# Four neighbouring heads to a chunk: q in one transfer, k in one and its last keys at the end of the tile

## The chip, the cores and the metric

The kernel runs on one core of one Trainium2 chip. The metric is the device time of one execution in microseconds. Several executions are timed; one more is recorded by the profiler, and the profile's numbers come from that one.

## What is computed

Attention with normalised q and k, and behind it two matrix products with a tanh-approximated GELU between them:

```python
q, k, v: (8, 12, 448, 64) float32        # batches, heads, positions, head size
q_n, k_n = rmsnorm(q, g_q), rmsnorm(k, g_k)
scores = q_n @ k_n.T / sqrt(64);  attn = softmax(scores)
x = (attn @ v).transpose(0, 2, 1, 3).reshape(3584, 768)
out = gelu_tanh(x @ w_in) @ w_out        # w_in (768, 2048), w_out (2048, 768)
```

## The kernel before

The work goes batch by batch. A batch has 12 heads, taken as three chunks of four heads; a chunk is two pairs of heads, and pair `hp = 2c + j` of chunk `c` is its even (`j = 0`) or odd (`j = 1`) pair. `head(c, j)` says which heads these are: before, heads 2c and 2c+1 for the even pair and 6+2c and 7+2c for the odd one.

For each chunk the kernel loads q and k (`load_q`, `load_k`, `loads`), squares them (`square`), sums the squares (`total`), makes the reciprocal root (`rsqrt`), scales (`normed`) and transposes. In q 112 partitions hold four positions each. Of k's 448 keys the first 384 lie three to a partition, and the last 64 are kept apart: those of the even pair on partitions 0 to 63, those of the odd pair on 64 to 127, in one place ("slot") of the tile. So a k tile holds 2 × 7 units of 64 numbers on each partition: three for each of the two even heads, three for each of the two odd heads, and the two last ones. v is loaded in the same split: `vb` holds the first 384 keys, `vr` the last 64, in two halves of 64 partitions (`load_v` parts 1 and 2) whose other half stays zero.

In batch 0 and for the first chunks of batch 1 TensorE transposes; later chunks are transposed by DMA (`dma_trans`, lines 281 and 285), and k is then multiplied by the product of the two gains (`gain`, line 291, on VectorE). Scores go to PSUM, ScalarE takes the exponential (L343), VectorE adds exponentials over key tiles (`key_sum`, L355 and L357), TensorE sums over keys with a matrix of ones and multiplies by v (L443, `x_couple` and `sums_couple`), and the normalised result lands in `xT`, one 128-row slab per pair. `mm1` multiplies `xT` by `win`; since pairs are not in the order of the model's columns, the slab of w_in for pair `c` is `c // 2 + NCH * (c % 2)`. GELU follows (L537), and `mm2` multiplies by `wout` (L443 and L557) and stores.

Every engine works through its queue in the order in which the program names the instructions. This order is written by hand. `FRONT` is the order up to the middle of batch 0's first product: `v1`, `v2`, `v0` load batch 0's v; `V0` to `V2` batch 1's; `w0` to `w3` the quarters of w_in; `o0` to `o3` those of w_out; `nq0:P` scales q of pair 0 on GpSimd, and so on. Behind it `STEPS` gives, batch by batch, the order of TensorE's work; while batch b's first product runs, batch b+1 is scaled on GpSimd and transposed, and the next loads are issued, at numbered places of that product:

```python
m1 += [(-1, lambda c=c: normed_all(b + 1, c)),
       (4 * c + 4, lambda c=c: transposed(b + 1, c))]
m1 += [(9, lambda: gain(b + 1, 0)), (13, lambda: gain(b + 1, 1))]
m1 += [(2, lambda: loads(b + 2, 1)), (6, lambda: loads(b + 2, 2))]
```

So on SyncE's queue, which also issues the stores, there stand in this order: loads (b+2, chunk 1), transposes of q and k (b+1, chunk 0), loads (b+2, chunk 2), transposes (b+1, chunk 1), transposes (b+1, chunk 2). GpSimd's queue holds the loads of v and of the weights beside its scaling and squaring; `load_v_piece` brings a later batch's v in five pieces, the last two of which are the halves of `vr`.

Of the kernel before, what the change touches and what calls it, by code (L numbers as in the profile page):

```python
# [8 lines left out]
F32 = mybir.dt.float32  # L9
# [3 lines left out]
AX = mybir.AxisListType  # L13
# [3 lines left out]
def kernel(  # L17
# [23 lines left out]
    NK = 3  # L41
# [68 lines left out]
        return slice(0, NK) if j == 0 else slice(NK, NS)  # L110

    def head(c, j):
        return 2 * c + HP * j

    def load_q(b, c):
        t = rawqk.tile([P, CH, NQ, D], F32, tag="rawq", name="rawq")
        raws["q", b, c] = t
        return [
            lambda j=j: nc.sync.dma_start(  # L119
                t[:, 2 * j:2 * j + 2],  # L120
                q[b, head(c, j):head(c, j) + 2].rearrange("h (p t) d -> p h t d", t=NQ),
            )
            for j in range(2)
        ]

    SM = 128 * NK

    def own(j):
        return slice(64 * j, 64 * j + 64)

    def load_k(b, c):
        t = rawqk.tile([128, 2, NS, D], F32, tag="rawk", name="rawk")
        raws["k", b, c] = t

        def main(j):
            h = head(c, j)
            nc.sync.dma_start(
                t[:, :, 4 * j:4 * j + NK],
                k[b, h:h + 2, :SM].rearrange("a (p t) d -> p a t d", t=NK),
            )  # L140

        def last(j):
            h = head(c, j)
            nc.sync.dma_start(t[own(j), :, NK], k[b, h:h + 2, SM:].rearrange("a p d -> p a d"))  # L144
        return [lambda: main(0), lambda: main(1), lambda: last(0), lambda: last(1)]

    def loads(b, c):
        lq, lk = load_q(b, c), load_k(b, c)
        for go in (lq[0], lk[0], lq[1], *lk[1:]):
            go()  # L150

    def load_v(b, part):
        if part == 0:
            nc.gpsimd.dma_start(
                vb[b % 2].rearrange("p h t d -> p h (t d)"),
                v[b, :, :SM].rearrange("h (p t) d -> p h (t d)", t=NK),
            )
        else:
            j = part - 1
            nc.gpsimd.dma_start(  # L160
                vr[b % 2][own(j), j], v[b, HP * j:HP * j + HP, SM:].rearrange("h p d -> p h d")
            )

    def load_v_piece(b, i):

# [6 lines left out]
            v[b, hs, :SM].rearrange("h (p t) d -> p h (t d)", t=NK),  # L172
        )

    def view(n, t, j=None):

        if n == "q":
            return t if j is None else t[:, 2 * j:2 * j + 2]
        return t if j is None else t[:, :, slots(j)]

    def sq_tile(n, flat):
        if n == "q":
            return flat[:P].rearrange("p (h t d) -> p h t d", h=CH, t=NQ)
        return flat[:, :2 * NS * D].rearrange("p (a s d) -> p a s d", a=2, s=NS)

    def square(b, c, n, eng, part=None):
        if (n, b, c) not in sqs:
            sqs[n, b, c] = sq_tile(n, sqp.tile([128, CH * NQ * D], F32, tag="sq", name="sq"))
        sq, raw = sqs[n, b, c], raws[n, b, c]
        if part is not None:  # L190
            if part[0] == "pair":
                sq, raw = view(n, sq, part[1]), view(n, raw, part[1])
            elif n == "q":
                sq, raw = view(n, sq, part[1]), view(n, raw, part[1])
            else:
                sq, raw = sq[:, part[1]], raw[:, part[1]]
# [5 lines left out]
    def stat(t, b, c, n, j=None):  # L202

        if b == 0:
            ns = NQ if n == "q" else NK + j
            at = 14 * j + (0 if n == "q" else 8)
            return t[:P if n == "q" else 128, c, at:at + 2 * ns].rearrange("p (a t) -> p a t", a=2)
        if n == "q":
            s = t[:P, c, :CH * NQ].rearrange("p (h t) -> p h t", h=CH)
            return s if j is None else s[:, 2 * j:2 * j + 2]  # L210
        s = t[:, c, CH * NQ:].rearrange("p (a s) -> p a s", a=2)
        return s if j is None else s[:, :, slots(j)]

    def total(b, c, n, j=None):
        nc.vector.reduce_sum(stat(ssq[b % 3], b, c, n, j), view(n, sqs[n, b, c], j), axis=AX.X)  # L215

    def rsqrt(b, c=slice(0, NCH), at=slice(0, NU)):
        if b not in rinvs:
# [12 lines left out]
    def normed(b, c, n, j, eng):  # L231
        if (n, b, c) not in nrms:
            shape = [P, 2, NQ, 2, D] if n == "q" else [128, NS, 2, D]
            nrms[n, b, c] = nrmp.tile(shape, BF16, tag=f"nrm{n}", name=f"nrm{n}")
        t = nrms[n, b, c]
        dst = t[:, j] if n == "q" else t[:, slots(j)]
        r = stat(rinvs[b], b, c, n, j)
        eng.tensor_mul(  # L238
            dst.rearrange("p t a d -> p a t d"), view(n, raws[n, b, c], j),
            r.to_broadcast(list(r.shape) + [D]),  # L240
        )

    def trans(b, hp, n, pool, tag=None):
        c, j = hp // 2, hp % 2
# [67 lines left out]
    def scores(b, hp, t, parts=1):  # L312

        c, j = hp // 2, hp % 2
        sc = place("sc")
        if t == "r":
            exrs[b, c] = exr.tile([128, 2, S], BF16, tag="exr", name="exr")
            for a in range(2):
                for jj in range(2):
                    r = slice(a * D, (a + 1) * D)  # L320
                    o = slice(64 * jj, 64 * jj + 64)
                    nc.tensor.matmul(  # L322
                        sc[o, a, :S], kT[r, c, NK, o], qT[b][r, 2 * c + jj],
                        start=True, stop=True,
                    )
            dst = exrs[b, c]
        else:
            if t == 0:
# [33 lines left out]
    def pair_products(b, hp, what, home=None, part=None):  # L362
# [5 lines left out]
        main = [exs[b, hp][:, t] for t in range(NK)]  # L368
        if what:
            steps = [(main[t], lambda a, t=t: vb[b % 2][:, head(c, j) + a, t]) for t in range(NK)]  # L370
            steps.append((exrs[b, c], lambda a: vr[b % 2][:, j, 2 * c + a]))
        elif b == 0:
            steps = [(e, lambda a: ones) for e in main] + [(exrs[b, c], lambda a: onesr[:, j])]
        else:
            steps = [(ess[b, hp], lambda a: ones)]
        if part is not None and j:
# [108 lines left out]
    def mm1_couple(b, fs, apart):  # L485
# [29 lines left out]
    def mm1(b, fs, cs=range(HP), parts=1, only=None, act=True):  # L515
# [8 lines left out]
        for j, f in enumerate(fs):  # L524
            m = 128 // parts
            for c in cs if only in (None, f) else ():
                for i in range(parts):
                    nc.tensor.matmul(  # L528
                        h[i * m:(i + 1) * m, j, :S],
                        win[:, c // 2 + NCH * (c % 2), f * 128 + i * m:f * 128 + (i + 1) * m], xT[b][:, c],  # L530
                        start=(c == 0), stop=(c == HP - 1),
                    )
        if cs[-1] == HP - 1 and only in (None, fs[-1]) and act:
# [282 lines left out]
    def front(step):  # L816
# [93 lines left out]
        y1 tpk0 v0 nq1:P ck0:D shift cq0:D s0 sq3:A e0 y3 s1 tq2 tq3 tk2 nk1:P L11 e1 y3 tpk1  # L910
        tpq1 s2 sk3:P w0 e2 ck1:D cq1:D tk3 y1 y1 s3 y3 y4 s4 sa0 rS1 nq2:P e3 sk4:A e4 sq4:D
        nk2:D s5 sb0 tpq2 s6 tpk2 tq4 tk4 st0 cq2:D rc0 ck2:D e5 sq5:P nk3:P nq3:D L12 e6 sa1 s7
        tpk3 tpq3 s8 sb1 e7 rs4 s9 xa0 sk5:P ck3:D rb0 cq3:D tk5 st1 e8 e9 xb0 s10 xt0 tq5 rc1
        rb1 nk4:P nq4:P e10 sa2 s11 rs5 e11 nk5:P nq5:P w1 xa1 sb2 xb1 s12 tpk4 tpq4 s13 Sq0:P
        Sk0:P e12 cq4:A st2 xt1 ck4:D rc2 rb2 e13 xa2 xb2 sa3 tpq5 tpk5 s14 e14 xt2 ck5:D cq5:D
        s15 xa3 sb3 e15 U xb3 s16 s17 s18 e16 st3 e17 rc3 rb3 xt3 e18 sa4 mb0 mb1 sb4 xa4 xb4
# [3 lines left out]
        Nq11:D Nk10:D Nq10:D Sq2:D Tk2 Tq2 Ck1:A g5 Cq1:A md6 md7 g6 g7 md8 g8  # L920
"""
    for step in FRONT.split():
        front(step)
# [174 lines left out]
```

## Time and profile before

| what | value |
|---|---|
| timed runs | 405.2, 405.5 and 404.85 us; median 405.2 |
| the profiled execution | 405.13 us, of which the span from the first to the last instruction is 403.3 |
| granted TensorE clock | 1.000 |
| TensorE busy | 392.3 us |
| ScalarE, VectorE, GpSimd busy | 305.6, 240.9, 138.4 us |
| moved by DMA | 54.65 MB |

The rows shown below come from several views. In the list of groups a row gives the line, engine, operation, what it writes and reads with its shape, the count, and after the bar the busy time in us and the mean duration in ns. In the order of time a row gives start and length in us; a bracket is the idle time ahead of it and what ended it. `SPq` is SyncE's queue issuing transfers. "DMA to landing" is the time from a transfer's issue until its data is there. A TensorE busy share near 100% does not by itself mean full speed, as the ends of matmuls are modelled; the count of matmuls in a stretch says more.

### The profile page before, as it was taken

What the parts mean: (1) busy time and instruction counts of PE and PEld (TensorE: products, weight loads), DVE (VectorE), ACT (ScalarE), POOL (GpSimd) and SP (SyncE); (2) the same over time, 40 slices, a digit from 0 to 9 for tenths busy, and PEclk for the clock granted to TensorE, in tenths of its full rate; (3) what the DMA queues carried; (4) which work ended last, traced back from release to release, by engine and by line L of the source; (5) the groups of instructions that cost most, each with busy time, mean ns of one, the idle gap of its engine ahead of it and who ended that gap; (6) DMA issues with size and microseconds to landing.
All of it is one profiled execution on the core that took longest, in us unless ns stands there. A gap on an engine that the chain in (4) does not pass through costs nothing.

```text
span 403.3 us, 17169 instructions
## 1 busy us (share of the span) xinstructions
PE 392.3 (97%) x7644; PEld 273.0 (68%) x7644; DVE 240.9 (60%) x406; ACT 305.6 (76%) x412; POOL 138.4 (34%) x155
## 2 busy tenths in 40 slices
PE   7899989999999999999999998999999999999996
PEld 3344557677777898766776666766787667966564
DVE  5989839987887437961498314973488411770010
ACT  4997889969997689885998479875998358964400
POOL 6878001252500764065603447037520740000000
PEclk9999999999999999999999999999999999999999
DMA  8999999998891599449981399918980290210022
GB/s 191 225 234 223 205 197 209 232 235 155 208 166 29 158 178 191 98 115 170 183 141 40 92 180 142 195 47 181 156 121 16 74 145 3 81 40 5 2 79 79
DMA packets 98090, 54.65 MB, mean 136 GB/s; under 512 B 63968, under 2 KB 94560, under 8 KB 98016
## 3 DMA queue, kind: packets, MB, share of 16 engines
q1 hardware_dynamic: 71392, 41.69, 47.3%
q0 software_dynamic: 26304, 11.80, 23.0%
q8 instruction: 59, 0.97, 1.0%
q14 instruction: 15, 0.12, 0.1%
q10 hardware_dynamic: 320, 0.07, 0.1%
HBM read 45.61 MB, written 11.01 MB: 140 GB/s over the span
## 4 chain that ended last, share of the span: by engine, by line
PE 88%; SPq 4%; DMA 2%; DVE 2%; ACT 2%; issue 1%; POOL 0%; ACTq 0%; DVEq 0%; POOLq 0%
PE hh L443 25%; PE om L443 16%; PE mm L443 12%; PE o L443 10%; PE sc L336 6%; PE o L557 5%; PE so L443 4%; PE hh L528 4%; PE ox L382 1%; DMA rawk<-in_k_dram 1%; DMA kT<-nrmk 1%; PE sc L322 1%; PE o L382 1%; SPq L285 1%; SPq L144 1%; SPq L119 1%
## 5 line engine op out<-in xcount | busy, mean ns | idle before, releaser
L343 ACT ACTIVATE ex<-sc,shift 128x896 bf16<-128x896 f32 x144 | 137.2, 1023 | 7.7 <-PE sc L336 6.2
L443 PE MATMUL hh<-xT,win 64*64 64x448 bf16 x2304 | 129.3, 349 | 0.0
L443 PEld LDWEIGHTS <-g 64*64 64x64 bf16 x3072 | 105.6, 107 | 27.4 <-issue 1.9
L443 PEld LDWEIGHTS <-win 64*64 64x64 bf16 x2688 | 87.0, 106 | 39.7 <-ACTq L452 10.3
L443 PE MATMUL om<-wout,g 64*64 64x384 bf16 x1664 | 105.0, 323 | 0.1
L443 PE MATMUL o<-wout,g 64*64 64x384 bf16 x704 | 83.0, 323 | 0.6 <-ACT g L537 0.6
L443 PE MATMUL mm<-wout,g 64*64 64x384 bf16 x704 | 83.2, 323 | 0.0
L537 ACT ACTIVATE g<-hh 128x896 bf16<-128x896 f32 x55 | 50.0, 916 | 26.3 <-PE hh L443 24.4
L215 DVE TENSOR_REDUCE ss<-sq 128x14 f32<-128x896 f32 (+4 forms) x45 | 47.8, 1078 | 19.3 <-ACT sq L198 16.9
L336 PE MATMUL sc<-qT,kT 64*64 64x448 bf16 (+1 forms) x540 | 54.8, 352 | 1.9 <-DVE qT L267 1.4
L238 POOL TENSOR_TENSOR nrmq<-rawq,rinv 112x512 bf16<-112x512 f32 x35 | 36.7, 1064 | 34.0 <-DMA qT<-nrmq 28.3
L291 DVE TENSOR_SCALAR kT<-kT,gcol 128x896 bf16<-128x896 bf16 x19 | 13.4, 707 | 51.5 <-DMA kT<-nrmk 51.5
L937 POOL COPY mark<-es 1x1 bf16<-1x1 bf16 x8 | 1.8, 225 | 115.3 <-DVE es L357 97.3
L238 POOL TENSOR_TENSOR nrmk<-rawk,rinv 128x512 bf16<-128x512 f32 (+1 forms) x34 | 31.8, 950 | 3.0 <-ACT rinv L224 2.1
L357 DVE TENSOR_TENSOR es<-ex 128x896 bf16<-128x896 bf16 x42 | 25.8, 614 | 11.7 <-ACT ex L343 11.7
L336 PEld LDWEIGHTS <-kT 64*64 64x64 bf16 (+1 forms) x540 | 23.5, 104 | 12.1 <-issue 4.1
L443 PE MATMUL o<-xT,win 64*64 64x448 bf16 x192 | 30.9, 349 | 0.0
L443 PE MATMUL mm<-xT,win 64*64 64x448 bf16 x192 | 30.9, 349 | 0.0
L357 DVE TENSOR_TENSOR es<-es,ex 128x896 bf16<-128x896 bf16 x42 | 26.0, 620 | 4.3 <-ACT ex L343 2.4
L343 ACT ACTIVATE exr<-sc,shift 128x896 bf16<-128x896 f32 x24 | 24.4, 1018 | 1.2 <-PE sc L322 1.0
L397 DVE STREAM_TRANSPOSE rb<-rc 128x448 f32<-128x448 f32 x34 | 21.9, 645 | 1.1
L443 PEld LDWEIGHTS <-vb 64*64 64x64 bf16 x504 | 16.6, 106 | 6.6 <-ACTq L452 0.8
(120 smaller groups left out, 525.6 us busy)
## 6 DMA issues: line engine op xcount, KB each, us to landing
rawq<-in_q_dram SPq DMA_DIRECT2D x48, 224.0 KB, 4.5
rawk<-in_k_dram SPq DMA_DIRECT2D x48, 192.0 KB, 4.9
vb<-in_v_dram POOLq DMA_DIRECT2D x18, 192.0 KB, 6.1
win<-in_moe_w_in_dram POOLq DMA_DIRECT2D x4, 768.0 KB, 10.8
wout<-in_moe_w_out_dram POOLq DMA_DIRECT2D x4, 768.0 KB, 19.6
out_dram<-osb SPq DMA_DIRECT2D x7, 336.0 KB, 3.4
out_dram<-osb SPq DMA_DIRECT2D x8, 288.0 KB, 2.8
out_dram<-osb SPq DMA_DIRECT2D x8, 240.0 KB, 2.6
```

What stands on the lines that cost most here:

```text
L215: nc.vector.reduce_sum(stat(ssq[b % 3], b, c, n, j), view(n, sqs[n, b, c], j), axis=AX.X)
L238: eng.tensor_mul(dst.rearrange("p t a d -> p a t d"), view(n, raws[n, b, c], j), r.to_broadcast(list(r.shape) + [D]),)
L291: nc.vector.tensor_scalar(kT[:, c], kT[:, c], gcol[:, 0:1], None, op0=ALU.mult)
L336: nc.tensor.matmul(sc[o, a, :S], kT[r, c, 4 * j + t, o], qT[b][r, hp], start=True, stop=True,)
L343: nc.scalar.activation(dst, sc[:, :, :S], AF.Exp, scale=scale, bias=shift)
L357: nc.vector.tensor_add(es, ex[:, 0] if t == 1 else es, ex[:, t])
L382: nc.tensor.matmul(o[a * D:(a + 1) * D], w(a), e[:, a], start=(i == 0), stop=(i + 1 == len(steps)),)
L397: nc.vector.transpose(oas["rb", hp], oas["rc"].to_broadcast([128, S // 32, 32]))
L443: self.last = nc.tensor.matmul(self.outs[k][own(m)], w, e, start=not self.begun[k], stop=self.left[k] == 0,)
L528: nc.tensor.matmul(h[i * m:(i + 1) * m, j, :S], win[:, c // 2 + NCH * (c % 2), f * 128 + i * m:f * 128 + (i + 1) * m], xT[b][:, c], start= ...
L537: nc.scalar.activation(g[:, fs[0]:fs[0] + len(fs), (b % 2) * S:(b % 2 + 1) * S], hs1[fs[0]][:, :, :S], AF.Gelu_apprx_tanh)
L557: nc.tensor.matmul(o[j * m:(j + 1) * m, :HD], g[:, f, i * 128 + j * m:i * 128 + (j + 1) * m], wout[:, f, half * HD:(half + 1) * HD], start ...
```

## The change

A chunk becomes four neighbouring heads, 4c to 4c+3, and pairs are now in the order of the model's columns, so `mm1` takes slab `c` of w_in. From batch 1 on, q of a chunk is one transfer instead of two, and the first 384 keys of k are one instead of two; the last keys remain two transfers and land behind the others at the end of the tile. Batch 0 keeps the two halves and its old layout. Tiles of raw values, squares and sums are addressed as flat runs of units (`units`, `flat`). As the last keys are no longer between the others, `normed` scales the odd pair's k from batch 1 on in two instructions (384 and 128 elements on a partition) instead of one of 512. The halves of `vr` take every second head of a chunk, so each half is loaded by two transfers instead of one. In `FRONT`, `v1` and `v2` move to the front of the order, and `V0 V1 V2` move behind `o2 o3`.

```diff
     def head(c, j):
-        return 2 * c + HP * j
+        return CH * c + 2 * j
...
     def load_q(b, c):
         t = rawqk.tile([P, CH, NQ, D], F32, tag="rawq", name="rawq")
         raws["q", b, c] = t
-        return [
-            lambda j=j: nc.sync.dma_start(
-                t[:, 2 * j:2 * j + 2],
-                q[b, head(c, j):head(c, j) + 2].rearrange("h (p t) d -> p h t d", t=NQ),
+
+        def some(lo, hi):
+            h = head(c, 0)
+            nc.sync.dma_start(
+                t[:, lo:hi], q[b, h + lo:h + hi].rearrange("h (p t) d -> p h t d", t=NQ)
             )
-            for j in range(2)
-        ]
+        return some
...
     def load_k(b, c):
-        t = rawqk.tile([128, 2, NS, D], F32, tag="rawk", name="rawk")
+        t = rawqk.tile([128, 2 * NS, D], F32, tag="rawk", name="rawk")
         raws["k", b, c] = t
+        odd = t[:, 2 * NK:].rearrange("p (a t) d -> p a t d", a=2)
+
+        def main(lo, hi):
+            h = head(c, 0)
+            dst = t[:, NK * lo:NK * hi].rearrange("p (a t) d -> p a (t d)", t=NK)
+            if (lo, hi) == (2, 4):
+                dst = odd[:, :, 1:].rearrange("p a t d -> p a (t d)")
+            nc.sync.dma_start(
+                dst, k[b, h + lo:h + hi, :SM].rearrange("a (p t) d -> p a (t d)", t=NK),
+            )
+
+        def last(j):
             h = head(c, j)
             nc.sync.dma_start(
-                t[:, :, 4 * j:4 * j + NK],
-                k[b, h:h + 2, :SM].rearrange("a (p t) d -> p a t d", t=NK),
+                odd[own(j), :, 0] if b == 0 else t[own(j), NK * CH:],
+                k[b, h:h + 2, SM:].rearrange("a p d -> p a d"),
             )
...
     def loads(b, c):
-        lq, lk = load_q(b, c), load_k(b, c)
-        for go in (lq[0], lk[0], lq[1], *lk[1:]):
-            go()
+        some, (main, last) = load_q(b, c), load_k(b, c)
+        for lo, hi in ((0, 2), (2, 4)) if b == 0 else ((0, 4),):
+            some(lo, hi)
+            main(lo, hi)
+        for j in range(2):
+            last(j)
...
             j = part - 1
-            nc.gpsimd.dma_start(
-                vr[b % 2][own(j), j], v[b, HP * j:HP * j + HP, SM:].rearrange("h p d -> p h d")
-            )
+            for a in range(2):
+                nc.gpsimd.dma_start(
+                    vr[b % 2][own(j), j].rearrange("p (c a) d -> p c a d", a=2)[:, :, a],
+                    v[b].rearrange("(c h) s d -> h c s d", h=CH)[2 * j + a, :, SM:].rearrange(
+                        "c p d -> p c d"),
+                )
...
-        t = nrms[n, b, c]
-        dst = t[:, j] if n == "q" else t[:, slots(j)]
-        r = stat(rinvs[b], b, c, n, j)
-        eng.tensor_mul(
-            dst.rearrange("p t a d -> p a t d"), view(n, raws[n, b, c], j),
-            r.to_broadcast(list(r.shape) + [D]),
-        )
+        t, r = nrms[n, b, c], stat(rinvs[b], b, c, n, j)
+        raw = flat(n, raws[n, b, c])[:, units(n, j)]
+        if n == "q":
+            parts = [(t[:, j], 0, NQ)]
+        elif b == 0:
+            parts = [(t[:, slots(j)], 0, NK + j)]
+        else:
+            parts = [(t[:, (NK + 1) * j:(NK + 1) * j + NK], 0, NK)]
+            parts += [(t[:, NK:NK + 1], 2 * NK, 1)] * j
+        for dst, lo, m in parts:
+            x, w = (y[:, lo:lo + 2 * m] for y in (raw, r))
+            w = w.rearrange("p (a t) -> p a t", t=m)
+            eng.tensor_mul(
+                dst.rearrange("p t a d -> p a t d"), x.rearrange("p (a t) d -> p a t d", t=m),
+                w.to_broadcast(list(w.shape) + [D]),
+            )
...
-                return win[own(r), c // 2 + NCH * (c % 2), at:at + 64], xT[b][own(r), c]
+                return win[own(r), c, at:at + 64], xT[b][own(r), c]
...
     FRONT = """
-        sk0:D v1 sq0:A tq0 tk0 rs0 gcol sk1:A sq1:D nq0:P v2 tq1 nk0:D tk1 rs1 sq2:A sk2:A tpq0
+        v1 v2 sk0:D sq0:A tq0 tk0 rs0 gcol sk1:A sq1:D nq0:P tq1 nk0:D tk1 rs1 sq2:A sk2:A tpq0 y1
...
-        s19 s20 Tq0 st4 rc4 rb4 sa5 mb2 Sk1:P w2 w3 e19 e20 GELU o0 Sq1:A xt4 Tk0 mb3 xa5 sb5
-        xb5 ma1 mc0 mc1 st5 o1 V0 V1 rc5 rb5 xt5 Tq1 Tk1 Sk2:D md0 md1 ma2 mc2 md2 g0 g1 EXP md3
-        Rs0 Nk00:D Nq01:D Nq00:D md4 Tp0 g2 g3 V2 o2 o3 Cq0:A g4 Nk01:D Ck0:A md5 Tp1 Nk11:D
+        sa5 mb2 Sk1:P w2 w3 e19 e20 GELU o0 Sq1:A xt4 Tk0 mb3 xa5 sb5 xb5 ma1 mc0 mc1 st5 o1 rc5
+        rb5 xt5 Tq1 Tk1 Sk2:D md0 md1 ma2 mc2 md2 g0 g1 EXP md3 Rs0 Nk00:D Nq01:D Nq00:D md4 Tp0
+        g2 g3 o2 o3 V0 V1 V2 Cq0:A g4 Nk01:D Ck0:A md5 Tp1 Nk11:D Nq11:D Nk10:D Nq10:D Sq2:D Tk2
```

More of the change, by code (lines that the diff above doesn't have):

```diff
@@ L112, in head, with own @@
     def head(c, j):
-        return 2 * c + HP * j
+        return CH * c + 2 * j
+    SM = 128 * NK
+    def own(j):
+        return slice(64 * j, 64 * j + 64)
     def load_q(b, c):
@@ L188, in square @@
             sqs[n, b, c] = sq_tile(n, sqp.tile([128, CH * NQ * D], F32, tag="sq", name="sq"))
-        sq, raw = sqs[n, b, c], raws[n, b, c]
+        sq, raw = sqs[n, b, c], flat(n, raws[n, b, c])
         if part is not None:
[L191 to L196, printed above, removed]
+            u = units(n, part[1])
+            if part[0] == "half" and n == "k":
+                u = slice(NS * part[1], NS * (part[1] + 1))
+            sq, raw = sq[:, u], raw[:, u]
         if eng is nc.scalar:
@@ L370, in pair_products @@
             steps = [(main[t], lambda a, t=t: vb[b % 2][:, head(c, j) + a, t]) for t in range(NK)]
-            steps.append((exrs[b, c], lambda a: vr[b % 2][:, j, 2 * c + a]))
+            steps.append((exrs.get((b, c)), lambda a: vr[b % 2][:, j, 2 * c + a]))
         elif b == 0:
-            steps = [(e, lambda a: ones) for e in main] + [(exrs[b, c], lambda a: onesr[:, j])]
+            steps = [(e, lambda a: ones) for e in main] + [(exrs.get((b, c)), lambda a: onesr[:, j])]
         else:
```

56 lines of the change are left out of this document (25 added, 31 removed).

## The prediction

> **What bounds the kernel now.** I read the page first, then the time of each engine in stretches of 5 us, then the chain of waits in the one stretch after start-up where TensorE stands, then SyncE's queue and the DMA traffic there. From the page:
>
> ```profile
> span 403.3 us, 17169 instructions
> PE 392.3 (97%) x7644; PEld 273.0 (68%) x7644; DVE 240.9 (60%) x406; ACT 305.6 (76%) x412; POOL 138.4 (34%) x155
> PE 88%; SPq 4%; DMA 2%; DVE 2%; ACT 2%; issue 1%; POOL 0%; ACTq 0%; DVEq 0%; POOLq 0%
> rawq<-in_q_dram SPq DMA_DIRECT2D x48, 224.0 KB, 4.5
> rawk<-in_k_dram SPq DMA_DIRECT2D x48, 192.0 KB, 4.9
> ```
>
> TensorE is busy 97% of the span and is 88% of the chain that ended last. So a cheaper load gains nothing by itself: only where TensorE stands still, and SyncE's queue (SPq, 4% of the chain) is why, is there time to win. The stretches show one such place after start-up (columns: busy time and instructions of PE, PEld, DVE, ACT, POOL, then clock, DMA share, GB/s):
>
> ```profile
> 245.00:250.00 5.00, 5.00 (x124) 4.14 (x120) 2.00 (x4) 5.00 (x7) 5.00 (x6) 1.00 1.09 127
> 250.00:255.00 5.00, 3.83 (x86) 2.62 (x82) 4.93 (x9) 3.67 (x5) 0.72 (x2) 1.00 1.33 227
> ```
>
> Between 250 and 255 us TensorE is busy for 3.83 of 5 us and runs 86 matmuls where the stretch before has 124. The list of waits names its cause, and the chain around it how it came about (start, length, what):
>
> ```profile
> PE mm L443 <- DVE es L357: 1.2, 1, 1.2
> 236.42 0.53 SPq L119
> ...
> 239.84 3.20 SPq L285
> ...
> 243.08 4.79 DMA kT<-nrmk
> ...
> 247.90 0.45 DVE kT L291
> 248.35 0.99 DVE ss L215
> ...
> 251.52 0.62 DVE es L357
> ...
> 252.19 0.38 PE mm L443 x2
> ```
>
> Read it from below. Batch 5's first sums over keys (PE mm, 252.19) wait 1.2 us for the last of four additions on VectorE (es, L357). VectorE works in order, and ahead of those additions stands the gain of batch 5's second chunk (kT, L291), which waits for that chunk's k transpose; this was issued at 243.08 and took 4.79. The transpose was late because SyncE's queue was still issuing loads for batch 6. The queue itself:
>
> ```profile
> 227.31 2.00 SPq L119 DMA_DIRECT2D rawq<-in_q_dram  x1
> 229.42 0.40 SPq L137 DMA_DIRECT2D rawk<-in_k_dram  x1
> 229.87 0.46 SPq L119 DMA_DIRECT2D rawq<-in_q_dram  x1
> 230.38 0.45 SPq L137 DMA_DIRECT2D rawk<-in_k_dram  x1
> 230.87 1.38 SPq L144 DMA_DIRECT2D rawk<-in_k_dram  x2
> 232.35 1.28 SPq L285 DMA_TRANSPOSE qT<-nrmq  x1
> 233.68 2.64 SPq L281 DMA_TRANSPOSE kT<-nrmk  x1
> ```
>
> Six issues (batch 6, chunk 1), two transposes (batch 5, chunk 0), six issues from 236.42 (batch 6, chunk 2), two transposes (batch 5, chunk 1). From the first to the kT transpose at 243.08 this takes 15.8 us.
>
> **The change, part by part.** The sum is made against the profiled execution's own 405.13 us (span 403.3 and 1.83 around it); the median of the three timed runs, 405.2, is the same within 0.1.
>
> *Fewer issues.* From batch 1 on a chunk has four issues instead of six: one of q and one of k's main part go. An issue and the step to the next are 0.45 to 0.51 us (229.42, 229.87, 230.38, 230.87), so 0.96 us per chunk if a merged transfer costs what a half costs. Is that so? The two L144 transfers (64 keys of two heads, 32 KB each) take 1.38 together, 0.69 each, and the 224 KB of L119 0.46: the issue does not grow with the bytes. Bounds for a merged issue: 0.46 and 0.92, the second by doubling. I take 0.46, as the small transfer is the dearer one. Ahead of the kT transpose lie two chunks, so 1.9 us of issuing go, at least 0.
>
> *How much of this reaches TensorE.* Not all, as the transfers must move too. The traffic there, by microsecond:
>
> ```profile
> 233.00:234.00 1.00, 1.00 (x29) 0.62 (x21) 0.00 (x0) 0.74 (x2) 0.00 (x0) 1.00 0.98 228
> 234.00:235.00 1.00, 1.00 (x28) 0.64 (x24) 0.00 (x0) 0.83 (x2) 0.00 (x0) 1.00 2.36 87
> 235.00:236.00 1.00, 1.00 (x28) 0.59 (x24) 0.00 (x0) 0.33 (x1) 0.00 (x0) 1.00 0.14 8
> 242.00:243.00 1.00, 1.00 (x32) 0.76 (x28) 0.00 (x0) 0.98 (x2) 0.00 (x0) 1.00 0.07 15
> ```
>
> A chunk is 2·224 + 2·192 + 2·32 = 896 KB, 918 thousand bytes; at the 228 GB/s of 233 to 234 us that is 4.0 us, about what six issues take (227.31's end at 229.31 to 232.25 is 2.9 for five). Behind each chunk the traffic falls to 8 or 15 GB/s for about a microsecond before transposes run, and the transposes' issues stretch (2.64, 3.20) meanwhile. So a part of the queue's time is the drain of the loads, and issuing sooner shortens only the head of it. I count 0.5 us per chunk, half of the 0.96, which is the middle between a pure issue limit and a pure drain limit: 1.0 us for two chunks, bounds 0 and 1.9. The stall is 1.2 (1.16 by the row of that matmul), and TensorE is dense behind it, so what is won there stays to the end. **Gain 1.0, from 0 to 1.2.** Late next, if kT lands that much sooner, is nothing of VectorE's: its four additions follow without it, and TensorE asks for them at 251.0.
>
> *k's scaling in two instructions.* From batch 1 on the odd pair's k is scaled as 384 elements and 128 elements instead of 512. By shape:
>
> ```profile
> L238 POOL TENSOR_TENSOR nrmk<-rawk,rinv 128x512 bf16<-128x512 f32 x18 | 18.9, 1049 | 2.1 <-ACT rinv L224 2.1
> L238 POOL TENSOR_TENSOR nrmk<-rawk,rinv 128x384 bf16<-128x384 f32 x16 | 13.4, 838 | 1.0 <-DMA rawq<-in_q_dram 1.0
> L238 DVE TENSOR_TENSOR nrmk<-rawk,rinv 128x384 bf16<-128x384 f32 x8 | 5.0, 625 | 1.4 <-ACT rinv L224 1.4
> L238 DVE TENSOR_TENSOR nrmk<-rawk,rinv 128x512 bf16<-128x512 f32 x6 | 4.0, 684 | 0.0
> 63.79 0.62 DVE L357 TENSOR_TENSOR es<-es,ex 128x896 bf16<-128x896 bf16 x1
> 64.85 0.38 PE L443 MATMUL so<-es,ones 64*64 64x448 bf16 x4
> ```
>
> 128 elements are not shown. GpSimd's line through its two rows gives 1049 − 3·211 = 416 ns, so a pair costs 838 + 416 − 1049 = 0.2 us more, between 0 and 0.84; 15 of them, all in GpSimd's idle two thirds: 0. On VectorE the line gives 684 − 3·59 = 507 ns, so 0.45 more at most and 0.1 at least, in six places. The tightest is batch 1's last chunk, just ahead of batch 1's additions: the last ends at 64.41 and TensorE asks at 64.85, a cover of 0.44 us. I take 0, at most 0.1.
>
> *v's last keys in two transfers per half, earlier and later.* At the start GpSimd issues four instead of one ahead of its first scaling. For batch 1, v's three loads move behind the last two of w_out on GpSimd's queue. Rows (a landing row belongs to the issue above it):
>
> ```profile
> 3.35 0.84 POOL L160 DMA_DIRECT2D vr<-in_v_dram  x1
> DMA to landing us min/median/max: 5.0/5.0/5.0
> 6.59 1.07 POOL L238 TENSOR_TENSOR nrmq<-rawq,rinv 112x512 bf16<-112x512 f32 x1 [2.41 <-ACT rinv L224]
> 35.69 1.05 POOL L154 DMA_DIRECT2D vb<-in_v_dram  x1
> DMA to landing us min/median/max: 19.5/19.5/19.5
> 40.92 0.88 POOL L783 DMA_DIRECT2D wout<-in_moe_w_out_dram  x1 [1.97 <-DMA win<-in_moe_w_in_dram]
> DMA to landing us min/median/max: 23.3/23.3/23.3
> 66.11 0.38 PE L443 MATMUL o<-ex,vb 64*64 64x448 bf16 x2
> ```
>
> Start: GpSimd idles 2.41 us before its scaling at 6.59, which waits for ScalarE. Three more issues at 0.84 make 2.5, so 0.1 at most on start-up; with half the rows each I take 0. The loads of batch 0 keep their order and count. Batch 1: v's main part lands at 55.2 now and is first used at 66.11; the last w_out part, now at the tail, lands at 64.2. The queue moves the same bytes, so v would land at about 64.2, and the cover falls from 11 to 1.9 us. The last w_out issue waited 1.97 us for a w_in part, and v's issues could wait likewise; this too comes out of the cover. I take 0; without cover each microsecond late costs one. In the other batches the two more issues per batch fall into GpSimd's idle time: 0. Scores, exponentials and products keep their instructions; heads are only renumbered, w_in's index with them: 0.
>
> Sum: 405.13 − 1.0 = 404.1, or **404.2** from the median.
>
> **Rivals.** *The drain sets it.* If the kT transposes start when the loads have drained, whatever the issue, kT lands as late as before but for the first transfers' few tenths. For it speak the 8 and 15 GB/s gaps and the stretched issues; against it that 235 to 236 and 242 to 243 are empty, not full. Gain 0 to 0.5: 404.9. [...] No row here yet separates the two.
>
> *The merge does not shorten the queue.* A merged issue at 0.92 leaves SyncE as it was: 405.1. Against it speaks the 0.69 for 32 KB.
>
> *v comes late.* The slower side: behind w_out the last rows of v meet batch 2's loads. Such a piece (3.35), among the first loads, needed 5.0 us to land. If the tail costs that behind 64.2, it lands at 69.2, 3.1 us after 66.11. The stall decides from 66.1 on and makes the kernel slower than before once it eats the gain, from 67.1; at 2 us, about the middle of what makes it slower than the runs can hide, the time is 404.2 + 2 = 406.2. For it: small pieces are now last in the queue; against it: batch 2's loads stand behind batch 1's transposes on SyncE. [...]
>
> **How the numbers follow.** Forecast (stall mostly gone, 403.9 to 404.5): 0.47. Drain: 0.30. No shorter queue: 0.06. v late: 0.17. A measurement of this kernel tells about 0.2%, 0.8 us, from no change. Of the forecast's 0.47 some 0.05 fall short of 0.8 us, and 0.01 of the drain passes it: faster 0.43. Same: 0.05 + 0.29 + 0.05 = 0.39. Slower: the late v and 0.01 for small delays where the queue is not shorter, 0.18. The range runs from the whole stall gone (405.2 − 1.2, less 0.3 for the runs' own spread) to the late v at 2 us, and leaves out the later half of that: 403.7 to 406.2.
>
> **What would show it.** Right: 4 issues per chunk in SyncE's queue at about 0.46 each; batch 5's kT landing before 246.8; no TensorE wait for es near 252, 250 to 255 with over 110 matmuls. Drain: fewer issues, but longer transposes' issues and the same landing. Wrong: merged issues of 0.9; a wait of o<-ex,vb or exr,vr near 66 us; es additions late near 64.4; start-up's first scaling after 6.7.

## The result and the profile after

The changed kernel takes 408.56 us in the median of 17 runs, the kernel before 405.5 in 17 runs between them: a ratio of 1.0065, 95% interval 1.0043 to 1.0087, so slower by 0.65% or 2.6 us (3.1 by the medians). A second comparison gave 1.0066 (1.0031 to 1.0101). The forecast was 404.2; no rival named what happened.

The page of the changed kernel, whose profiled execution took 409.1 us:

```profile
span 407.3 us, 17158 instructions
PE 393.9 (97%) x7644; PEld 273.2 (67%) x7644; DVE 242.7 (60%) x412; ACT 305.9 (75%) x412; POOL 149.9 (37%) x186
q8 instruction: 60, 0.98, 1.0%
PE 89%; DVE 3%; DMA 3%; issue 2%; ACT 2%; SPq 0%; POOL 0%; ACTq 0%; DVEq 0%; POOLq 0%
rawq<-in_q_dram SPq DMA_DIRECT2D x21, 448.0 KB, 5.6
rawk<-in_k_dram SPq DMA_DIRECT2D x21, 384.0 KB, 6.5
```

SyncE's queue has left the chain (SPq 4% to 0%; the kernel before, profiled a second time further down, has 1%). In its place stands more "issue", which is time in which an engine waited for nothing that the profile shows. Loads take longer to land: 5.6 and 6.5 us where the halves took 4.5 and 4.9. The stretch that the prediction was about is full now, 122 products where there were 86:

```profile
250.00:255.00 5.00, 5.00 (x122) 4.05 (x114) 3.11 (x6) 5.00 (x7) 3.46 (x6) 1.00 1.26 241
```

The loss is elsewhere. In order of time TensorE stands still five times, each time with "issue" in the bracket; the profile before has no wait of TensorE over 0.15 us with that name (one of 0.12 stands at 204.84 us). Four of the five:

```profile
78.49 0.51 PE L465 MATMUL om<-wout,g 64*64 64x384 bf16 x5 [0.75 <-issue]
86.06 1.24 PE L465 MATMUL hh<-xT,win 64*64 64x448 bf16 x20 [1.23 <-issue]
116.23 0.35 PE L465 MATMUL mm<-wout,g 64*64 64x384 bf16 x2 [1.06 <-issue]
163.12 0.38 PE L358 MATMUL sc<-qT,kT 64*64 64x448 bf16 x3 [0.86 <-issue]
```

With one of 0.33 at 255.51 these are 4.2 us. Less the 1.2 us that the old stall near 252 took, 3.0 are left; the two profiled executions differ by 4.0. A bracket counts from the end of the last product, and products last 0.32 to 0.35 us where four new ones start every 0.16 us (122 in 5 us); so by an estimate from these numbers a stall, the old one too, costs some 0.17 us more than its bracket, and 3.7 of the 4.0 are accounted for.

What is common to the five is seen when the instructions that TensorE has executed by then are counted. Stretches from 0 to the start of each stall; PE and PEld are the first two counts:

```profile
0.00:77.74 77.74, 72.76 (x863) 40.16 (x863) 61.24 (x119) 65.62 (x93) 39.34 (x54) 1.00 1.23 217
0.00:84.82 84.82, 79.09 (x991) 44.01 (x991) 65.82 (x126) 69.86 (x100) 41.66 (x57) 1.00 1.23 222
0.00:115.18 115.18, 108.22 (x1630) 66.19 (x1630) 90.02 (x164) 95.46 (x132) 54.31 (x68) 1.00 1.12 207
0.00:162.26 162.26, 154.24 (x2653) 104.41 (x2653) 115.81 (x206) 133.65 (x185) 76.00 (x95) 1.00 1.01 188
0.00:255.18 255.18, 246.29 (x4698) 170.61 (x4699) 173.23 (x294) 208.37 (x285) 117.00 (x145) 1.00 0.91 169
```

863 + 863 = 1726, then 1982, 3260, 5306 and 9397. Divided by 256 the remainders are 190, 190, 188, 186 and 181. These counts leave out what TensorE's sequencer runs: two instructions at the start and the semaphore instructions of two lines of the program.

```profile
L358 PEldq EVENT_SEMAPHORE  x12: 51/51/51, 101.0 to 345.7; - x12
L344 PEldq EVENT_SEMAPHORE  x4: 51/51/51, 68.4 to 353.6; - x4
```

With those that have run by then, 3, 3, 5, 7 and 12, the remainder is 193 each time: every stall stands at the same place of a block of 256 instructions. The queue "q8 instruction" of the page has 60 packets and 0.98 MB, 16 KB each; TensorE's 2 · 7644 = 15288 instructions are 59.7 blocks of 256. So, read from these counts, the queue brings TensorE's program, one packet a block, and TensorE has run dry at the end of a block, for 4.2 us in this execution.

How late a fetch starts can be read too. The packets of q8 that start at 83.59 and at 98.98 us, against the executed instructions:

```profile
0.00:83.59 83.59, 77.86 (x972) 43.49 (x976) 64.73 (x124) 68.74 (x98) 40.43 (x56) 1.00 1.23 219
0.00:98.98 98.98, 92.03 (x1264) 54.55 (x1268) 75.55 (x140) 79.71 (x112) 46.54 (x59) 1.00 1.13 210
```

At 98.98, in a stretch with fewer loads (104 GB/s from 94.70 to 99.00 us, 257 from 78.50 to 83.60), 2532 instructions are done: 38 past the last block end (2494). At 83.59 it is 1948, 222 past the last block end (1726) and 34 short of the next. The packet takes 1.1 us and so ends at 84.65; TensorE reaches the block's end at 84.82 and goes on at 86.06, 1.4 us after the packet. So in this trace a block is fetched about one block ahead, and its instructions run only some time after the packet's end. Read in the same way, the fetches before the five stalls started 190, 222, 200, 202 and 161 instructions late, and the stalls end 1.35 to 1.65 us after their packets. The remainder is 193 again, with the sequencer's instructions, at the 13 stalls of four profiles further down: 3 of the changed kernel's second profile, 2 of the second of the kernel before, 4 with the shift and 4 with halves only in the burst. Of the other fetches of the changed kernel's first profile and of the first of the kernel before none started more than 173 late; that one (202.54 us, before) came ahead of the 0.12 us at 204.84, and one 166 late (161.81, before) brought no wait. The same two fetches (starting at 75.02 and 80.87) in the kernel before:

```profile
0.00:80.87 80.87, 74.86 (x936) 42.06 (x939) 64.73 (x119) 68.41 (x97) 35.74 (x48) 1.00 1.21 215
0.00:75.02 75.02, 69.01 (x804) 38.21 (x808) 59.19 (x111) 62.89 (x89) 35.08 (x47) 1.00 1.20 213
```

They started 149 and 142 late and were just in time. The old kernel stood at the edge without showing it.

**Theory.** SyncE has at most eight transfers under way: of the 240 issues in the trace of the kernel before and the 198 in that of the changed one none starts while more than seven others have yet to land, 38 and 30 start with exactly seven, and in the changed kernel even a store waits for a k load that it does not read, in the list of waits.

```profile
SPq L607 <- DMA rawk<-in_k_dram: 3.4, 3, 2.2
```

Eight of the new transfers (448, 384, 32, 32 KB and again) are 1.8 MB, eight of the old ones at most 1.3 MB (a chunk's six, 896 KB, and two more halves, 416 KB). By the theory the larger amount under way delays the fetches. Rivals: v's additional transfers and the new order at the start; the layout and the divided scaling; the size of the single transfer rather than the bytes under way.

### The profile page after: what moved, and what is told of

Same layout as the page of the kernel before. It is cut to its first block, busy times and chain, and to the rows that moved or that the text cites. A ratio compares the mean times of both kernels' runs of the same rounds, so it can differ in the third digit from the quotient of the medians.

```text
span 407.3 us, 17158 instructions
## 1 busy us (share of the span) xinstructions
PE 393.9 (97%) x7644; PEld 273.2 (67%) x7644; DVE 242.7 (60%) x412; ACT 305.9 (75%) x412; POOL 149.9 (37%) x186
## 4 chain that ended last, share of the span: by engine, by line
PE 89%; DVE 3%; DMA 3%; issue 2%; ACT 2%; SPq 0%; POOL 0%; ACTq 0%; DVEq 0%; POOLq 0%
PE hh L465 27%; PE om L465 15%; PE mm L465 13%; PE o L465 10%; PE sc L358 7%; PE o L579 4%; PE so L465 4%; PE hh L550 4%; DMA rawk<-in_k_dram 3%; PE ox L404 1%; PE sc L344 1%; PE o L404 1%; ACT ex L365 1%; DVE es L377 1%; DVE ss L228 1%
## 5 line engine op out<-in xcount | busy, mean ns | idle before, releaser
L465 PEld LDWEIGHTS <-win 64*64 64x64 bf16 x2688 | 88.5, 106 | 40.0 <-ACTq L474 10.5
L559 ACT ACTIVATE g<-hh 128x896 bf16<-128x896 f32 x55 | 49.9, 916 | 26.4 <-PE hh L465 24.4
L358 PE MATMUL sc<-qT,kT 64*64 64x448 bf16 (+1 forms) x540 | 56.0, 352 | 3.1 <-DVE qT L289 1.3
L313 DVE TENSOR_SCALAR kT<-kT,gcol 128x896 bf16<-128x896 bf16 x19 | 15.2, 800 | 38.1 <-DMA kT<-nrmk 38.1
L260 POOL TENSOR_TENSOR nrmk<-rawk,rinv 128x384 bf16<-128x384 f32 (+2 forms) x49 | 34.1, 717 | 2.2 <-ACT rinv L237 1.7
L358 PEld LDWEIGHTS <-kT 64*64 64x64 bf16 (+1 forms) x540 | 23.8, 104 | 13.8 <-issue 6.0
L172 POOL DMA_DIRECT2D vr<-in_v_dram x32 | 20.6, 656 | 21.2 <-PE so L465 11.4
## 6 DMA issues: line engine op xcount, KB each, us to landing
win<-in_moe_w_in_dram POOLq DMA_DIRECT2D x4, 768.0 KB, 12.3
```

Of the source, the lines that this page charges most:

```text
L172: nc.gpsimd.dma_start(vr[b % 2][own(j), j].rearrange("p (c a) d -> p c a d", a=2)[:, :, a], v[b].rearrange("(c h) s d -> h c s d", h=CH)[2 ...
L260: eng.tensor_mul(dst.rearrange("p t a d -> p a t d"), x.rearrange("p (a t) d -> p a t d", t=m), w.to_broadcast(list(w.shape) + [D]),)
L313: nc.vector.tensor_scalar(kT[:, c], kT[:, c], gcol[:, 0:1], None, op0=ALU.mult)
L358: nc.tensor.matmul(sc[o, a, :S], kT[r, c, 4 * j + t, o], qT[b][r, hp], start=True, stop=True,)
L465: self.last = nc.tensor.matmul(self.outs[k][own(m)], w, e, start=not self.begun[k], stop=self.left[k] == 0,)
L559: nc.scalar.activation(g[:, fs[0]:fs[0] + len(fs), (b % 2) * S:(b % 2 + 1) * S], hs1[fs[0]][:, :, :S], AF.Gelu_apprx_tanh)
```

## The experiments

Stall sums below are TensorE's waits with "issue" of over 0.15 us in the one profiled execution; ratios are to the kernel before in the same comparison.

**Undo only the merge: halves.** Everything else of the change stays; the first line keeps the new layout of k behind batch 0, and every later run with halves of k has it too.

```diff
-            if (lo, hi) == (2, 4):
+            if b == 0 and (lo, hi) == (2, 4):
...
-        for lo, hi in ((0, 2), (2, 4)) if b == 0 else ((0, 4),):
+        for lo, hi in ((0, 2), (2, 4)):
```

> The changed kernel, but q and k of a chunk are loaded in two halves in every batch, as before the change (six load issues a chunk instead of four); the new layout, the two-instruction scaling of k, v's last keys in two transfers per half and the new order at the start all stay. Theory (the merged loads put more bytes in front of TensorE's instruction fetches, which then come late): the stalls of TensorE that the profile puts down to issue, 4.2 us in all in the changed kernel, shrink to under 1.5 us, load landings return from 5.6 and 6.5 to about 4.5 and 4.9 us, the wait for es near 252 comes back (about 1 us), and the time is about 405.5, ratio to the kernel before 1.000 +- 0.002. Rival A (v's extra transfers and the new order at the start cost it): the stalls between 70 and 93 us stay (about 2 us) and the time is 408 or more, since the gain at 252 is lost as well. Rival B (layout and the split scaling cost it): 408 or more with no stalls put down to issue.

Ratio 1.0004 (0.9977 to 1.0030), stalls 0.86 us (0.36 and 0.50), landings 4.8 and 5.1 us. The merge is the cause; v's transfers, the layout, the scaling and the order together cost nothing that can be measured. One expectation failed: with the old six issues the wait for es did not come back. That sent the next question to the kernel before.

**The kernel before, profiled again.**

> The kernel before, profiled once more, to see which of its stalls come back. If the stall for es near 252 is a steady cost of its queue: 0.8 to 1.4 us again. If it is one execution's chance (the run with halves has the same six issues and did not show it): under 0.4 us or gone. Stalls put down to issue: 0 to 1 us.

404.64 us in the one execution, and its list of waits names no es. These two of its rows carry "issue":

```profile
PE hh L443 <- issue: 0.9, 1, 0.9
PE so L443 <- issue: 0.6, 1, 0.6
```

The stall on which the whole forecast rested was one execution's chance. The two stalls of the other kind sum to 1.55 us (at 7·256 + 190 and 21·256 + 186). So the old kernel pays now and then what the new one pays more often.

**The changed kernel again.**

> The changed kernel once more, profiled and timed beside the others. Theory: ratio 1.004 to 1.009; stalls put down to issue of 2.5 to 5 us in all, each at 256 n + 181 to 190 executed instructions, most at the same blocks as in the first profile (6, 7, 12, 20, 36). If the stalls of the first profile were one execution's chance: under 1.5 us, or at other blocks.

Ratio 1.0066, stalls 2.6 us in a profiled execution of 407.07 us (median 409.51): 0.62, 0.68 and 1.30 at blocks 6, 7 and 20, remainders 190, 190, 186. Those at 12 and 36 were missing. Block ends are fixed, which of them is late varies.

**Shift TensorE's program against its work.**

```diff
-    idle(20, ps_m.tile([128, 512], F32, tag="mm", name="w")[:, :S])
+    idle(84, ps_m.tile([128, 512], F32, tag="mm", name="w")[:, :S // 4])
```

> The changed kernel, but the 20 dummy products at the very start (448 columns each, TensorE has nothing to do there) are 84 dummy products of 112 columns: 64 more, so TensorE's stream of instructions is shifted by 128 against its work. Theory (the stalls stand at the ends of blocks of 256 instructions, where the next block has not been fetched): counted in executed PE and PEld instructions the stalls stay at 256 n + 186 to 190, that is at other products than before, 128 instructions earlier in the work; none stands at the old products. Rival (something in the work itself, a wait that the profile does not show, holds these products): they stay at the same products, at 256 n + 58 to 62 in the shifted count. Time 407 to 410 by either, since the number of boundaries is the same.

The stretches from 0 to the start of each stall in the shifted kernel:

```profile
0.00:81.27 81.27, 75.32 (x991) 45.40 (x991) 64.06 (x122) 68.32 (x97) 39.74 (x54) 1.00 1.23 216
0.00:203.00 203.00, 196.49 (x3675) 138.02 (x3676) 146.21 (x248) 169.74 (x233) 97.02 (x120) 1.00 0.98 180
0.00:244.16 244.16, 236.96 (x4571) 166.37 (x4571) 171.13 (x286) 200.11 (x276) 110.71 (x137) 1.00 0.93 168
0.00:255.64 255.64, 248.02 (x4826) 176.09 (x4827) 178.52 (x299) 211.21 (x289) 117.50 (x145) 1.00 0.95 170
```

Counts 1982, 7351, 9142, 9653: remainders 190, 183, 182, 181, with the sequencer's instructions 193 each time, although each product now has 128 more instructions ahead of it. The stalls stay with the ends of blocks and leave their products, so nothing in the work holds them. They sum to 2.0 us, the ratio is 1.0025 (0.9997 to 1.0054); the median, 407.0, is the lowest that was expected.

**Old order at the start.** `FRONT` of the kernel before, all else changed.

> The changed kernel with the order at the start as before the change: v's last keys and v's three loads for batch 1 go back to their places in GpSimd's queue; all loads of q and k stay merged. Theory (merged q and k loads make the fetches late): the time stays at 408 to 409 and stalls put down to issue stay between 70 and 93, near 115 and near 160 us, at 3 to 4 us in all. Rival A (order at the start and v's loads): the 2 us of stalls between 70 and 93 go and the time falls to about 406; those near 115 and 160 us stay.

Ratio 1.0110 (1.0073 to 1.0146). Stalls with "issue" stay (3.5 us), and named waits are added: 1.5 us for a w_out part, 0.5 for v, 0.4 for a w_in part. The order is not the cause; with merged loads the new order seems the better one, which I had not expected (408 to 409 us was expected here, 410.32 measured).

**One part alone: only q merged.**

```diff
-        for lo, hi in ((0, 2), (2, 4)) if b == 0 else ((0, 4),):
-            some(lo, hi)
-            main(lo, hi)
+        if b:
+            some(0, 4)
+        for lo, hi in ((0, 2), (2, 4)):
+            if b == 0:
+                some(lo, hi)
+            main(lo, hi)
```

> The changed kernel with only q merged from batch 1 on: q in one transfer, then k in two halves and the two last ones, five issues a chunk. Theory: between halves (1.0004 of the kernel before) and the changed kernel (1.0065): 1.002 to 1.005, stalls put down to issue of 1 to 3 us. Rival (the merged k with its three runs a head into one tile is the culprit): as with halves, 0.998 to 1.002.

Ratio 1.0035 (0.9997 to 1.0074), stalls 1.4 us at blocks 6, 7, 12 and 20: between the two by the point estimate, though the interval holds both ends.

**Halves only in the burst of batch 2's loads.**

```diff
-        for lo, hi in ((0, 2), (2, 4)) if b == 0 else ((0, 4),):
+        for lo, hi in ((0, 2), (2, 4)) if b in (0, 2) or (b, c) == (3, 0) else ((0, 4),):
```

> The changed kernel, but the four chunks whose loads stand in one burst between about 62 and 78 us (batch 2's three and batch 3's first) are loaded in halves; all others stay merged. Theory (a stall comes from the loads that stand in front of that block's fetch): the stalls at blocks 6 and 7 (near 78 and 86 us; 2.0 and 1.3 us together in the two profiles of the changed kernel) fall to under 0.7 us together, the one at block 20 or 21 (near 162) stays at 0.8 to 1.4 us, and the ratio lies between halves and the changed kernel, 1.001 to 1.005. Rival (the merge costs in some other way that goes with the whole kernel): all stalls as in the changed kernel, 1.005 to 1.009.

Ratio 1.0020 (0.9985 to 1.0054). The stall at block 6 is gone, the one at 7 is not (0.95; expected under 0.7 for both), those at 12, 20 and 36 stay (0.53, 0.65, 0.69; 0.8 to 1.4 was expected at 20). In one execution this is half of what was expected; the kernel before had 0.94 at block 7 as well.

**Bytes under way or size of the transfer?** Four runs were meant for it. First, merged loads and the last keys in four transfers:

```diff
+            if b:
+                for a in range(2):
+                    nc.sync.dma_start(t[own(j), NK * CH + a], k[b, h + a, SM:])
+                return
...
-                odd[own(j), :, 0] if b == 0 else t[own(j), NK * CH:],
-                k[b, h:h + 2, SM:].rearrange("a p d -> p a d"),
+                odd[own(j), :, 0], k[b, h:h + 2, SM:].rearrange("a p d -> p a d"),
```

> The changed kernel with q and k merged, but from batch 1 on the last keys in four transfers of one head each instead of two of two heads, so that a chunk has six issues again, two large and four small. If what counts is how many bytes stand in flight (SyncE has at most eight transfers under way, which are about 1.8 MB in the changed kernel, 1.2 MB before and here): stalls put down to issue fall below 1.5 us and the time is about 405.5 to 406. If the size of the single transfer counts (a fetch waits behind a long one): stalls stay at about 4 us and the time at 408.5 or above. Rival A (v's transfers and the order at the start): the stalls between 70 and 93 us stay, 408 to 409.

Ratio 1.0047 (1.0018 to 1.0077), profiled stalls 0.46. This run does not part the two as was meant: my 1.2 MB was wrong, since eight transfers in a row (q, k, four small, q, k) still hold 1.7 MB. With 1.7 MB the theory would have expected the stalls of the changed kernel. The profiled execution has far less, though it took 406.21 us where the median is 407.92, and the timed runs are slower than the kernel before all the same. Then two kernels with ten issues a chunk, one with the last keys in eight pieces, one with q and k by single heads:

```diff
+            if b:
+                for a in range(2):
+                    for i in (0, 32):
+                        nc.sync.dma_start(
+                            t[64 * j + i:64 * j + i + 32, NK * CH + a],
+                            k[b, h + a, SM + i:SM + i + 32],
+                        )
+                return
...
```

> The changed kernel with q and k merged, but from batch 1 on the last keys in eight transfers (one head, 32 rows each), so that a chunk has ten issues, two large and eight small. Eight transfers in a row, the most that SyncE has under way, then hold one chunk's q and k at most (about 0.87 MB), where in the changed kernel they hold two chunks' (1.8 MB) and in the run with four last transfers still 1.7. To be read beside the run with quarters, which has ten issues a chunk too. If the bytes under way make the fetches late: stalls put down to issue under 1 us in all, and the time equals that of the quarters within 0.3%. If the size of the single transfer does it: stalls of 2 us and more, 1 to 2.5 us slower than the quarters. By both, SyncE has 2.5 us more of issuing a chunk than with six issues, so transposes come later and a wait for es near 252 of 1 to 3 us may be added to both alike.

```diff
-        for lo, hi in ((0, 2), (2, 4)) if b == 0 else ((0, 4),):
+        for lo, hi in ((0, 2), (2, 4)) if b == 0 else [(i, i + 1) for i in range(CH)]:
```

> The changed kernel with q and k of a chunk loaded head by head from batch 1 on (four transfers of 112 KB and four of 96 KB, and the two last ones: ten issues a chunk). Eight transfers under way hold 0.83 to 0.85 MB. Theory (loads ahead of the fetches): stalls put down to issue fall to under 0.5 us, less than with halves (0.9), load landings under 4.5 us; the time would be 404.5 to 406 if SyncE's four extra issues a chunk stay hidden, and 407 to 408 if they bring back a wait for es near 252. Rival (fetch lateness has nothing to do with how the loads are cut): stalls of 2 to 4 us, 408 or more.

The eight pieces take 448.48 us (ratio 1.0993, 1.0923 to 1.1064), the quarters 439.81 (1.0843, 1.0794 to 1.0891), far beyond what was expected, and not equal to each other, as they would be by the bytes under way alone. Stalls with "issue" all but vanish (0.19 and 0), but so does the basis of the comparison: TensorE now waits elsewhere, which by my reading gives the fetches time. The chain of the quarters, where TensorE had 88% before and 94% with halves:

```profile
PE 57%; DMA 23%; SPq 10%; DVE 4%; POOL 2%; ACT 2%; issue 2%; ACTq 0%; POOLq 0%; DVEq 0%
```

Four more issues in 21 chunks are 84, at about 0.47 us 39 us; the run lost about 33 to the halves, a part of it as longer busy time of TensorE (405.3 against 394.8 us, at granted clocks of 0.972 and 0.992). SyncE's queue, from which two issues a chunk could be taken without any gain, has no room for four more. Last, halves again, with the last keys issued by GpSimd from batch 2 on, so that SyncE's eight are all halves:

```diff
-            nc.sync.dma_start(
+            (nc.gpsimd if b > 1 else nc.sync).dma_start(
```

> Halves again, but from batch 2 on the two last-key transfers of a chunk are issued by GpSimd. SyncE then has four issues a chunk, all of halves, so that the eight it has under way are two chunks (1.7 MB), as with the merged loads (1.8), while no single transfer is larger than before. If the bytes under way make TensorE's fetches late: stalls put down to issue of 1.5 to 4 us and a ratio of 1.003 to 1.007, as in the changed kernel. If the size of the single transfer does: stalls under 1 us and 1.000 +- 0.003, as with halves. A wait for GpSimd or for the last keys would show by its own name and is no evidence for either.

417.69 us (ratio 1.0307, 1.0265 to 1.0350), mostly by waits that carry other names (7.3 us for GELU, L559). But between 60 and 130 us its list of waits has only the two stalls at block ends, so the burst from 62 to 86 us can be compared: DMA traffic there of the changed kernel, of the halves and of this kernel, in that order.

```profile
DMA packets 10682, 6.08 MB, mean 253 GB/s; under 512 B 6501, under 2 KB 10341, under 8 KB 10677
...
rawq<-in_q_dram SPq DMA_DIRECT2D x4, 448.0 KB, 7.7
rawk<-in_k_dram SPq DMA_DIRECT2D x4, 384.0 KB, 8.7
```

```profile
DMA packets 10716, 5.12 MB, mean 213 GB/s; under 512 B 6933, under 2 KB 10711, under 8 KB 10711
...
rawq<-in_q_dram SPq DMA_DIRECT2D x8, 224.0 KB, 5.8
rawk<-in_k_dram SPq DMA_DIRECT2D x8, 192.0 KB, 6.6
```

```profile
DMA packets 10844, 6.04 MB, mean 252 GB/s; under 512 B 6671, under 2 KB 10517, under 8 KB 10840
...
rawq<-in_q_dram SPq DMA_DIRECT2D x8, 224.0 KB, 7.6
rawk<-in_k_dram SPq DMA_DIRECT2D x8, 192.0 KB, 7.5
```

Small transfers, packed as densely as the merged ones, move as much (252 GB/s), land nearly as late (7.6 and 7.5 us against 7.7 and 8.7), and bring stalls at blocks 6 and 7 of 0.74 and 0.40 us; the changed kernel has 0.75 and 1.23, then 0.62 and 0.68, the halves 0.36 and none. At first sight that speaks for the bytes under way and against the size. But single executions scatter too much for it: with halves in this burst the kernel before has 0 and 0.94 us here in its two profiles and the run with halves only in the burst 0.95, and with merged loads the run with four last transfers has none. Over the whole execution the 1.15 us of this kernel lie between the 1.5 to 4 that was expected by the bytes and the under 1 by the size. So it is the merge that brings the stalls (4.2 and 2.6 us with it, 0.86 with halves); whether by the bytes under way or by the size of its transfers stays open.

**Halves and the shift together.**

> Halves as in the first run, and the 64 more dummy products at the start that shift TensorE's stream by 128 instructions. If the place of the block ends is worth something by itself (0.4% lay between the changed kernel and its shifted form): 0.996 to 1.000 of the kernel before, and any stalls at 256 n + 181 to 190 of the executed instructions. If what the shift gave there came only with merged loads, or was chance: 1.000 +- 0.002, as without the shift.

Ratio 1.0016 (0.9984 to 1.0048), stalls 1.5 us. Where the block ends fall is worth nothing that can be measured here by itself. No version beat the kernel before.

**Stalls and time together.** Ten profiled executions have no large wait of another name: two each of the kernel before and the changed one, halves, shift, both together, only q, four last transfers, and halves in the burst. The six whose stalls sum to less than 1.6 us took 404.6 to 406.2 us, the four with 2.0 to 4.2 took 406.6 to 409.1.

## Why the prediction was wrong, point by point

**Issues of about 0.46 us, four a chunk: right** (behind the start-up the medians are 0.53 us for q and 0.45 for k's main part). The queue became shorter by about what was counted. The changed kernel's queue for batch 6's and 5's chunks, and VectorE's gain that the landing releases:

```profile
231.66 0.40 SPq L126 DMA_DIRECT2D rawq<-in_q_dram  x1
232.17 0.56 SPq L143 DMA_DIRECT2D rawk<-in_k_dram  x1
...
243.21 1.29 SPq L303 DMA_TRANSPOSE kT<-nrmk  x1
```

```profile
248.49 0.51 DVE L313 TENSOR_SCALAR kT<-kT,gcol 128x896 bf16<-128x896 bf16 x1 [3.14 <-DMA kT<-nrmk]
```

From the first issue to the second kT's issue it is 11.6 us, 15.8 before; to the gain 16.8, 20.6 before. But the 15.8 were a long stretch of one execution. The second profile of the kernel before has 12.4 at the same place, and its kT lands after 16.8 as well:

```profile
228.49 0.41 SPq L119 DMA_DIRECT2D rawq<-in_q_dram  x1
...
240.88 2.14 SPq L281 DMA_TRANSPOSE kT<-nrmk  x1
```

Over the five such stretches of each profile the mean is 14.2 and 13.8 us before, 14.4 with halves, and 12.3 and 12.2 with merged loads; to kT's landing it is 19.2 and 17.9, 18.5, and 17.2 and 17.0. So the 1.9 us of issuing do go, and on average the landing comes sooner, by 0.7 to 2.2 us: the rivals "the drain sets it" and "the merge does not shorten the queue" fall. Yet kT is used at 248.49, not before 246.8: everything starts 4.35 us later, as TensorE had by then lost 3.9 us to the first four stalls.

**Gain 1.0: the term that failed first.** It priced a stall seen in a single execution as a steady cost. It was not there in the second profile of the same kernel, nor in the halves, with or without the shift, which have the same six issues.

**"TensorE is dense behind it": the step that failed with the larger sum.** The prediction asked what a sooner issue would collide with only for v and for the transposes. The cover of TensorE's own program was not counted: 59 packets, 1.0% of the DMA time, in a queue of their own, needed by the engine that has no slack. Its cost stood at nothing without naming what hides it: a lead of about one block of 256 instructions (the packet at 98.98 us started 38 past a block's end), of which the same burst in the kernel before had already used up to 149. In its place the runs show 2.6 and 4.2 us of stalls at block ends in the two profiles of the changed kernel, against 0 and 1.55 before, and all of the loss gone with halves (1.0004).

**v's loads, the divided scaling, start-up: right at nothing** (halves: 1.0004). No wait for vb or vr stands near 66 us in the changed kernel, and the slower side came by a way that no rival described.

**The upper end of the range.** The range allowed a loss only by v. A merged transfer doubles the bytes per issue (448 KB of q for 224) where the traces have at most eight under way; with that, a rise of the landing times (4.5 to 5.6 and 4.9 to 6.5 us) and a cost for the other queues on the same DMA engines, among them the one that brings TensorE's program (1.0% of their time), would have been a rival.

## What to carry to other kernels

In this kernel, with TensorE busy 97% of the span, its instruction fetches were one more stream with a deadline, missed for 4.2 and 2.6 us in the two profiles of the changed kernel: count executed PE and PEld instructions, and the sequencer's, at a stall that the profile puts down to issue, and see whether the remainders by 256 agree. SyncE's queue had at most eight transfers under way here, of 224 KB or of 448; the bigger ones put more under way (1.8 MB against at most 1.3) and landed 1.1 and 1.6 us later; so look at landing times before and after, not only at issue costs. A stall of 1 us in one profile is worth a second profile before a change is made for it.

## What the runs showed of the hardware

- TensorE's program comes in 16 KB packets (60 in the changed kernel, 0.98 MB, for 59.7 blocks of 256 instructions), about one block ahead: the packet at 98.98 us started 38 instructions past a block's end. Fetches that started 190 to 222 instructions late left TensorE standing 0.75 to 1.23 us.
- After such a packet's end it took 1.35 to 1.65 us until TensorE, where it stood waiting, ran the block's first instruction (the five stalls of the changed kernel's first profile).
- Such a packet itself took mostly 0.9 to 1.4 us, in and out of bursts (at most 2.1 before and 2.2 in the changed kernel); what grew under load is the time until it started, from 38 instructions past a block's end at 104 GB/s to 222, or about 5 us, at 257 GB/s. Why loads in another queue keep it waiting that long is open.
- SyncE's queue is a cliff on one side only: two issues a chunk fewer than the halves' six gave nothing, four more by single heads cost about 33 us (439.81 against 406.64).
